# Hash attention and an MLP-mixer on one core: the token stage's last stores, weight chunks and last place

## The chip, the cores and the metric

The kernel runs on one core of a Trainium2 chip, in one launch. The metric is the device time of an execution in microseconds (us). Engines are called PE (TensorE), DVE (VectorE), ACT (ScalarE), POOL (GpSimd) and SP (SyncE, which here only issues DMAs).

## The reference

Four batches, eight heads, 768 positions, 64 features a head, float32. Queries and keys are put into buckets by six sign bits, and a query attends only to the keys of its bucket. The heads are then laid side by side to x (4, 768, 512), and an MLP-mixer follows: a token stage over the positions, and a channel stage over the features.

```python
def _attn_ref(q, k, v, proj):
    ...
    mask = q_bucket[:, :, :, None] == k_bucket[:, :, None, :]
    scores = scale * np.matmul(q, k.transpose(0, 1, 3, 2))
    scores = np.where(mask, scores, -1000000000.0)
    ...
    return np.matmul(attn, v)

def _moe_ref(x, w_tok1, w_tok2, w_ch1, w_ch2):
    xt = x.transpose(0, 2, 1)
    h = np.maximum(xt @ w_tok1, 0.0) @ w_tok2      # 768 -> 256 -> 768
    u = x + h.transpose(0, 2, 1)
    h2 = np.maximum(u @ w_ch1, 0.0) @ w_ch2        # 512 -> 1536 -> 512
    return (u + h2)
```

## The kernel before, in words

**Attention** (0 to 290 us) goes over 16 pairs of heads, four a batch. Its result is `XT`, the residual: 128 partitions, four blocks of features, 4 × 768 positions. The token stage also needs x with the positions on the partitions. So each pair's result is transposed by DVE and written to a DRAM buffer of its batch, `bounced[b]`, by `bounce` (L228): two transposes (L233) and four stores on SP's queue (L238). `fetch(b, x)` (L243) reads a batch back, on SP too (L245). There are two tiles for it: `x0` for batches 0 and 2, `x1` for 1 and 3. Most pairs are stored while attention still runs. The last pair of batch 2 is stored by `bounce_late` (L972) at the very end of attention, from a tile `raw`; on SP these four stores stand between `fetch_turned` (L929) and the fetch of `x1` for batch 1. The last pair of batch 3 is stored at the start of the token stage.

**The token stage** (`tokens`, 290 to 368 us) runs this for each batch b:

- `mix1(b)`: two times six matmuls of 128x512 (L1211) give relu(xᵀ·w_tok1), copied out of PSUM by ACT with the relu (L1218) to `r1`; behind each of the two, one `job()`.
- at b = 0, `weight_sums` (L1188 to L1191), and for every b `left_sums(b)` (L1234 to L1237): sums on DVE for the second product.
- from b = 1 on, the second product of the batch before, in two parts: `mix2(b-1, 0)`, a `job()`, `mix2(b-1, 1)`. Behind the loop come `mix2(3, 0)`, the first two sums of the channel stage (`inputs(0, T, 0)`, L1163 and L1164) and `mix2(3, 1)`.

`mix2(b, m)` (L1240) is one level of Strassen's scheme in seven products (L1251, 128x384), which PE writes to four PSUM banks. ACT copies four of the results to SBUF (L1256, L1259, L1261, L1263), and five adds on DVE (L1266 to L1270) finish the part in a *place*: `places` are three stretches of the weight buffer `second1`, taken in turn by `(2*b+m+1) % 3`. POOL then issues a DMA that adds the place to `XT` in memory (L1271, the accumulate-DMA, 768 KB). A place may be written again when its accumulate-DMA has read it.

A `job()` is mostly a *chunk*: one piece of the channel stage's weights, given as pairs of 32-bit words, is turned into float32 (`Conversion.one`): ACT L177, DVE L187, L191, L195, L196 and L206, and then SP fetches a further piece (L169). The tile `size` that L177 writes has two buffers, so that the L177 of a chunk waits for the L206 of the chunk two before. The first job makes weight sums on DVE (L1301 to L1306).

**The channel stage** (`channels`, 368 us to the end) takes three blocks of 1024 positions; `hidden(s, t)` (L1338 and on) makes a sixth of the hidden layer of a block, again in seven products. Its PSUM tiles `b0` to `b3` are two banks each. In a `hidden`, the first products go to `b0` or `b2` and its neighbour; ACT copies the first result (L1344), and PE then adds a third product to the same bank. DVE's L1378 and L1379 make `R0` from it, then DVE and POOL work on sums for later blocks (L1843 to L1846, the like of L1301 to L1306, and L1382 on POOL), and a last copy by ACT (L1344, the fourth) is followed by three adds (L1387) and L1353.

The order of each engine's instructions is the order in which the code issues them; a tile pool decides which buffer or bank a new tile takes, and puts in the waits for its earlier users. `x0` lies in SBUF over a stretch that the channel stage uses again for `R0` and `R1`; `x1` lies over tiles of attention that its last matmuls (L470) read.

Of the kernel before, what the change touches and what calls it, by code (L numbers as in the profile page):

```python
# [36 lines left out]
F32 = mybir.dt.float32  # L37
# [11 lines left out]
def kernel(  # L49
# [16 lines left out]
    nc = tc.nc  # L66
    P = 128
    B, NP, _, _, S = qk.shape
# [25 lines left out]
    NREG = B * NP - len(SORTED)  # L94
# [46 lines left out]
    class Conversion:  # L141
# [14 lines left out]
        def fetch(self):  # L156
            if not self.todo:
                return
            w, dst, rows, j, n = self.todo.pop(0)
            cols = NW // rows  # L160
            wv = (w.bitcast(U32) if double else w).rearrange("(j p) c -> p j c", p=P)
            src = wv[:, j : j + rows, NE * n : NE * (n + cols)]
            to = dst[:, j : j + rows, n : n + cols]
            if not double:
                nc.sync.dma_start(out=to, in_=src)
                self.fetch()
                return
            raw = self.pool.tile([P, NW, 2], U32, name="raw", tag="raw", bufs=self.bufs)
            nc.sync.dma_start(out=raw.rearrange("p (t n) w -> p t (n w)", t=rows), in_=src)  # L169
            self.fetched.append((raw, to, rows))  # L170
# [54 lines left out]
    dram = ctx.enter_context(tc.tile_pool(name="dram", bufs=1, space=bass.MemoryType.DRAM))  # L225
    bounced = [dram.tile([S, DM], F32, name=f"bounced{b}") for b in range(B)]

    def bounce(stage, n):  # L228

        b, hp = pairs[n]  # L230
        stage = stage.rearrange("p (a k i) -> p a k i", k=2, i=32)
        for k in range(2):
            nc.vector.transpose(  # L233
                stage[:, :, k], XT[:, hp + k, S * b : S * b + S].rearrange("p (a i) -> p a i", i=32),
            )
        to = bounced[b].rearrange("(a i) (g c) -> g i a c", i=32, g=4)
        for g in range(4):
            nc.sync.dma_start(  # L238
                out=to[g, :, :, 32 * hp : 32 * hp + 64],
                in_=stage[32 * g : 32 * g + 32].rearrange("p a k i -> p a (k i)"),  # L240
            )
# [5 lines left out]
    def turn(b, x, bank):  # L247

        for r in range(0, NR, 2):
            ps = bank()  # L250
            for k in range(2):
                at = S * b + P * (r + k)
                for cb in range(NCB):
                    nc.tensor.transpose(ps[:, k, P * cb : P * cb + P], XT[:, cb, at : at + P], ident)
            nc.scalar.copy(x[:, r : r + 2], ps)


    def attention(pool, psum, W1, W2, x0):
# [320 lines left out]
        n = 2 * W * SLOTS  # L579
# [15 lines left out]
        for name, w in widths.items():  # L595
            made[name] = sorting[:, sum(a.shape[1] for a in made.values()) :][:, :w]
        upto, every, pick = (made[name].bitcast(BF16) for name in ("upto", "every", "pick"))
        group_of, groups, place, beyond, spread, some, work, copy, least = (
            made[name]
            for name in ("group_of", "groups", "place", "beyond", "spread", "some", "work", "copy", "least")  # L600
        )
# [369 lines left out]

        def bounce_late():  # L972
            raw = pool.tile([P, NW, 2], U32, name="raw", tag="raw", bufs=2)
            bounce(raw.rearrange("p n w -> p (n w)").bitcast(F32), NREG - 4)

        at(NREG - 1, "newton", bounce_late)
        at(NREG - 1, "begin", fetch_turned)
# [192 lines left out]
    def tokens(pool, psum, W1, W2, x0, weights, jobs, T, places):  # L1170

        x1 = pool.tile([P, NR, DM], F32, name="x1", tag="x1", bufs=1)
        R1 = {}
        turned = not jobs
        if not turned:
            fetch(1, x1)  # L1180
            jobs = jobs(weights(pool))
            bounce(places[2], NREG - 2)
        NQ = DM // 2
        sums = pool.tile([P, 3, HALF], F32, name="W2sums", tag="W2sums", bufs=1)
        b00, b01, b10, b11 = (W2[:, k, HALF * n : HALF * n + HALF] for k in range(2) for n in range(2))

        def weight_sums():
            nc.vector.tensor_tensor(sums[:, 0], b01, b00, op=ALU.subtract)  # L1188
            nc.vector.tensor_tensor(sums[:, 1], b11, sums[:, 0], op=ALU.subtract)
            nc.vector.tensor_tensor(b01, b11, b01, op=ALU.subtract)  # L1190
            nc.vector.tensor_tensor(sums[:, 2], b10, sums[:, 1], op=ALU.subtract)  # L1191

        def job():
            if not turned and jobs:
                jobs.pop(0)()

        def bank(name):
            return psum.tile([P, 512], F32, name=name, tag="mm", bufs=4 if turned else 8)

        def banks():  # L1200
            return psum.tile([P, 2, 512], F32, name="trp", tag="tr", bufs=2)

        def mix1(b):
            x = (x0, x1)[b % 2]
            if b and turned:
                turn(b, x, banks)
            r1 = pool.tile([P, NJ, DM], F32, name="r1", tag="r1", bufs=2)
            for j in range(NJ):
                ps = bank("t1")
                for r in range(NR):  # L1210
                    nc.tensor.matmul(  # L1211
                        ps, W1[:, r, P * j : P * j + P], x[:, r], start=(r == 0), stop=(r == NR - 1),
                    )
                to = r1[:, j]
                if not turned:
                    to = to.rearrange("p (c g i) -> p g c i", c=NCB, i=32)
                    ps = ps.rearrange("p (g c i) -> p g c i", c=NCB, i=32)
                nc.scalar.activation(to, ps, ACT.Relu)  # L1218
                job()
            if b % 2:  # L1220
                new = pool.tile([P, 3, NQ], F32, name="r1s", tag="r1s", bufs=1)
            else:
                new = T[0].rearrange("p k t -> p (k t)")[:, : 3 * NQ].rearrange("p (i c) -> p i c", i=3)
            R1[b] = r1, new
            if not turned and b + 2 < B:
                fetch(b + 2, x)

        def left_sums(b):
            r1, new = R1[b]
            a00, a01, a10, a11 = (  # L1230
                r1[:, k].rearrange("p (m i c) -> p i m c", m=2, i=2)[:, i] for i in range(2) for k in range(2)
            )
            new = new.rearrange("p i (m c) -> p i m c", m=2)
            nc.vector.tensor_tensor(new[:, 1], a00, a10, op=ALU.subtract)  # L1234
            nc.vector.tensor_tensor(a10, a10, a11, op=ALU.add)
            nc.vector.tensor_tensor(new[:, 0], a10, a00, op=ALU.subtract)
            nc.vector.tensor_tensor(new[:, 2], a01, new[:, 0], op=ALU.subtract)  # L1237

        def mix2(b, m):

            r1, new = R1[b]
            a00, a01, s1, a11 = (
                r1[:, k, P * (2 * m + i) : P * (2 * m + i) + P] for i in range(2) for k in range(2)
            )
            new = new[:, :, P * m : P * m + P]
            ps = [bank("t2")[:, :HALF] for _ in range(4)]
            to = places[(2 * b + m + 1) % 3].rearrange("p (i n t) -> p i n t", i=2, n=2)
            p1, u, p7, p57 = (to[:, i, n] for i in range(2) for n in range(2))

            def product(at, left, right, start=True):  # L1250
                nc.tensor.matmul(  # L1251
                    ps[at], left, right, start=start, stop=True, skip_group_check=True,
                )

            product(0, a00, b00)
            nc.scalar.copy(p1, ps[0])  # L1256
            product(1, a01, b10)
            product(2, s1, sums[:, 0])
            nc.scalar.copy(p57, ps[2])  # L1259
            product(3, new[:, 1], b01)  # L1260
            nc.scalar.copy(p7, ps[3])  # L1261
            product(0, new[:, 0], sums[:, 1], False)
            nc.scalar.copy(u, ps[0])  # L1263
            product(2, new[:, 2], b11, False)
            product(3, a11, sums[:, 2], False)
            nc.vector.tensor_tensor(p1, ps[1], p1, op=ALU.add)  # L1266
            nc.vector.tensor_tensor(p57, p7, p57, op=ALU.add)
            nc.vector.tensor_tensor(p57, p57, u, op=ALU.add)
            nc.vector.tensor_tensor(p7, ps[3], u, op=ALU.add)
            nc.vector.tensor_tensor(u, ps[2], u, op=ALU.add)  # L1270
            nc.gpsimd.dma_start(  # L1271
                out=XT[:, 2 * m : 2 * m + 2, S * b : S * b + S], in_=to.rearrange("p i n t -> p i (n t)"),
                accum_op=ALU.add,
            )

        for b in range(B):
            mix1(b)
            if b == 0:
                weight_sums()
            left_sums(b)  # L1280
            if b:
                mix2(b - 1, 0)
                job()
                mix2(b - 1, 1)
        mix2(B - 1, 0)
        inputs(0, T, 0)
        mix2(B - 1, 1)
        while not turned and jobs:
            job()
# [926 lines left out]
    n = NHT // 4 * P  # L2216
# [139 lines left out]
```

## Time and profile before

| what | value |
|---|---|
| device time, median of three runs (lowest to highest) | 768.44 us (768.34 to 770.82) |
| the profiled execution: device time, span | 768.42 us, 766.7 us |
| TensorE's granted clock, mean | 0.999 |
| busy share of the span: PE, DVE, ACT, POOL | 99%, 88%, 58%, 24% |
| token stage, from its first to its last matmul | 289.90 to 368.4 us |

The span is the time from the first to the last instruction; 1.7 us of the execution lie around it. Rows of the profile give the start and the length in us, the engine and line, the operation, output<-inputs with the shapes, and xN where N instructions are put together. A bracket shows how long the engine was idle ahead of it and what ended that. Matmuls are pipelined, so that rows of PE overlap a little. Lines are those of the kernel before; from L1245 on the changed kernel's are three higher.

### The profile page before, as it was taken

To read this page: it belongs to the slowest core of one execution; us is meant where nothing else is said; L and a number is where in the kernel's file an instruction comes from. 1 tells how busy PE (TensorE), PEld (TensorE's weight loads), DVE (VectorE), ACT (ScalarE), POOL (GpSimd) and SP (SyncE) were. 2 spreads that over 40 slices of the span, in tenths; PEclk is the share of its full clock that TensorE was granted. 3 is DMA by queue.
4 is the path that set the end of the run, shared out by engine and by line. 5 is a ranking of instruction groups with operands and counts; after the bars stand their busy time and mean duration, and the time that the engine had idled before them with its cause. 6 is when DMAs were issued, how large, how long until landed. Compare 5 with 4: busy or idle time off the path is not lost.

```text
span 766.7 us, 14567 instructions
## 1 busy us (share of the span) xinstructions
PE 759.4 (99%) x5549; PEld 509.4 (66%) x5549; DVE 672.9 (88%) x965; ACT 444.5 (58%) x820; POOL 185.0 (24%) x258
## 2 busy tenths in 40 slices
PE   9999999999999999999999999999999999999997
PEld 4555655665656554455444468888877888886886
DVE  5899899999998888999788798998899799889884
ACT  6677777677777763334232326566766666665331
POOL 2346772647761700011220100100000011000001
PEclk9999999999999999999999999999999999999999
DMA  7746587674955548886696997899576696750555
GB/s 256 272 170 178 175 245 221 209 205 142 227 191 117 170 64 250 303 189 113 112 327 232 350 354 268 245 242 270 175 221 210 232 261 138 240 158 7 204 159 133
DMA packets 131210, 157.80 MB, mean 206 GB/s; under 512 B 56000, under 2 KB 99520, under 8 KB 129216
## 3 DMA queue, kind: packets, MB, share of 16 engines
q1 hardware_dynamic: 119248, 136.05, 55.9%
q0 software_dynamic: 11600, 20.53, 13.2%
q8 instruction: 45, 0.74, 0.4%
q10 hardware_dynamic: 288, 0.25, 0.1%
q14 instruction: 29, 0.24, 0.1%
HBM read 107.71 MB, written 40.67 MB: 194 GB/s over the span
## 4 chain that ended last, share of the span: by engine, by line
PE 84%; DVE 10%; ACT 2%; issue 1%; DMA 1%; POOL 1%; DVEq 0%; SPq 0%; ACTq 0%; POOLq 0%
PE b L1338 51%; PE sc L503 14%; PE acc L470 12%; PE sc L425 1%; PE hash L536 1%; PE ss L848 1%; DVE size L196 1%; ACT exps L414 1%; DVE unit L195 1%; PE sacc L874 1%; DMA XT<-second 1%; DVE esd L459 1%; DVE second L206 1%; DVE size L191 1%; PE ssums L862 1%
## 5 line engine op out<-in xcount | busy, mean ns | idle before, releaser
L414 ACT ACTIVATE exps<-sc 128x768 f32<-128x768 f32 (+1 forms) x181 | 126.7, 765 | 9.3 <-PE sc L503 6.6
L1338 PE MATMUL b<-R,second 128*128 128x256 f32 (+1 forms) x522 | 131.8, 408 | 0.0
L503 PE MATMUL sc<-qk 32*128 32x384 f32 (+1 forms) x1352 | 119.6, 457 | 0.0
L1338 PEld LDWEIGHTS b<-R,second 128*128 128x128 f32 x522 | 99.1, 190 | 28.5 <-issue 16.5
L470 PE MATMUL acc<-exps,vn 128*32 128x385 f32 (+1 forms) x1344 | 113.2, 486 | 0.0
L503 PEld LDWEIGHTS sc<-qk 32*128 32x128 f32 x1352 | 92.1, 185 | 16.6 <-issue 4.4
L470 PEld LDWEIGHTS acc<-exps,vn 128*32 128x32 f32 x1344 | 44.7, 109 | 62.7 <-issue 59.7
L1344 ACT COPY c<-b 128x256 f32<-128x256 f32 (+1 forms) x96 | 40.3, 426 | 79.4 <-PE b L1338 66.1
L376 POOL DMA_DIRECT2D bits<-XT x104 | 54.5, 526 | 71.2 <-issue 38.8
L459 DVE TENSOR_TENSOR esd<-esd,exps 128x768 f32<-128x768 f32 x70 | 66.9, 956 | 4.3
L1338 PE MATMUL b<-XT,WC 128*128 128x256 f32 (+1 forms) x208 | 61.0, 428 | 0.0
L791 POOL DMA_INDIRECT table<-XT,sorting x48 | 56.4, 1175 | 14.9 <-issue 13.5
L2048 POOL DMA_DIRECT2D out<-second x7 | 8.5, 1212 | 187.3 <-DVE second L2042 81.6
L1338 PEld LDWEIGHTS b<-XT,WC 128*128 128x128 f32 x208 | 39.5, 190 | 15.4 <-issue 10.3
L503 PE MATMUL sc<-bits 32*128 32x384 bf16 (+1 forms) x338 | 48.0, 311 | 0.1
L557 ACT COPY rec<-rec 32x384 f32<-32x384 f32 x56 | 28.5, 510 | 32.6 <-DVE rec L551 31.1
L1338 PE MATMUL b<-XT,SW 128*128 128x256 f32 (+1 forms) x164 | 47.0, 410 | 0.0
L455 DVE TENSOR_TENSOR esd<-esd,exps 128x768 f32<-128x768 f32 x42 | 40.2, 958 | 4.4
L1211 PE MATMUL t<-x,W 128*128 128x512 f32 x96 | 42.1, 594 | 0.1
L1338 PEld LDWEIGHTS b<-XT,SW 128*128 128x128 f32 x164 | 31.1, 190 | 9.4 <-issue 4.1
L1271 POOL DMA_DIRECT2D XT<-second x8 | 9.9, 1234 | 103.5 <-DVE unit L187 63.8
L1211 PEld LDWEIGHTS t<-x,W 128*128 128x128 f32 x96 | 18.1, 190 | 23.1 <-issue 21.7
(331 smaller groups left out, 1449.1 us busy)
## 6 DMA issues: line engine op xcount, KB each, us to landing
second<-left SPq DMA_DIRECT2D x20, 768.0 KB
qk<-in_qk_rows SPq DMA_DIRECT2D x13, 1152.0 KB
raw<-in_moe_w_ch SPq DMA_DIRECT2D x16, 768.0 KB
second<-left SPq DMA_DIRECT2D x18, 576.0 KB
WC<-hidden_left SPq DMA_DIRECT2D x18, 448.0 KB
x<-bounced SPq DMA_DIRECT2D x4, 1536.0 KB
XT<-second POOLq DMA_DIRECT2D x8, 768.0 KB
seen<-in_qk SPq DMA_DIRECT2D x15, 384.0 KB
```

Source lines behind the costliest of these rows:

```text
L376: nc.gpsimd.dma_start(out=to[at : at + 2 * BITS, half[j]], in_=g[of : of + 2 * BITS])
L414: return nc.scalar.activation(e[:, :, columns], sc, ACT.Exp, scale=SCALE)
L455: nc.vector.tensor_tensor(self.d, self.d, e, op=ALU.add)
L459: nc.vector.tensor_tensor(self.d, self.d, e, op=ALU.add)
L470: made = nc.tensor.matmul(acc[D * i + d : D * i + d + 32], vn[:, i, c, d : d + 32], e[:, i], start=(c == 0), stop=(c == NR - 1),)
L503: nc.tensor.matmul(made[j, piece][:, i], k[at : at + 32, ks], q[at : at + 32], start=part < 0, stop=part == 1,)
L557: nc.scalar.copy(rec[other : other + 32, h], rec[at : at + 32, h])
L791: nc.gpsimd.indirect_dma_start(out=tables[2 * w + i], out_offset=bass.IndirectOffsetOnAxis(ap=self.at[:, x : x + 1], axis=0), in_=row, in_ ...
L1211: nc.tensor.matmul(ps, W1[:, r, P * j : P * j + P], x[:, r], start=(r == 0), stop=(r == NR - 1),)
L1271: nc.gpsimd.dma_start(out=XT[:, 2 * m : 2 * m + 2, S * b : S * b + S], in_=to.rearrange("p i n t -> p i (n t)"), accum_op=ALU.add,)
L1338: nc.tensor.matmul(ps, left(k), right(k), start=start and k == ks[0], stop=stop and k == ks[-1], skip_group_check=True,)
L1344: nc.scalar.copy(c, ps)
```

## The change

Three edits. The four stores of `bounce_late` are issued on POOL's queue and not on SP's. The `job()` between the two parts of a second product moves behind both. And the last part, `mix2(3, 1)`, takes the tile `x0` as its place, a fourth one; `x0` is last read by `mix1(2)`.

```diff
-    def bounce(stage, n):
+    def bounce(stage, n, queue=nc.sync):
...
         for g in range(4):
-            nc.sync.dma_start(
+            queue.dma_start(
                 out=to[g, :, :, 32 * hp : 32 * hp + 64],
...
-            bounce(raw.rearrange("p n w -> p (n w)").bitcast(F32), NREG - 4)
+            bounce(raw.rearrange("p n w -> p (n w)").bitcast(F32), NREG - 4, nc.gpsimd)
...
-            to = places[(2 * b + m + 1) % 3].rearrange("p (i n t) -> p i n t", i=2, n=2)
+            place = places[(2 * b + m + 1) % 3]
+            if b + 1 == B and m:
+                place = x0.rearrange("p r c -> p (r c)")[:, : 2 * S]
+            to = place.rearrange("p (i n t) -> p i n t", i=2, n=2)
...
             if b:
                 mix2(b - 1, 0)
+                mix2(b - 1, 1)
                 job()
-                mix2(b - 1, 1)
         mix2(B - 1, 0)
         inputs(0, T, 0)
         mix2(B - 1, 1)
```

**On SP**, at the end of attention, the difference of the two programs (the rows are line, operation, output<-input, shape and count; `bounced_90` is batch 2, `x_3793` is `x1`):

```order
 L918 DMA bounced_91<-XT 128x6x32 x4
 L929 DMA stage<-bounced_91 32x24x32 x8
-L238 DMA bounced_90<-raw 32x24x64 x4
 L245 DMA x_3793<-bounced_89 128x6x512
 L169 DMA raw<-in_moe_w_ch 128x3x512 x2
```

The four stores are gone from ahead of the fetch of `x1`; they stand on POOL between its last gather of attention and the first accumulate-DMA. The fetch of `x0` for batch 2 waits for all four of them.

**On ACT**, from the end of part (0,0) to the first copy of part (1,0), before (`size` and `raw` are the tiles of a chunk, `t2` PSUM banks, `second1` the places):

```order
L177 ACTIVATE size_3910<-raw_3863 128x768
L1256 COPY second1_3784<-t2_3920 128x384
L1259 COPY second1_3784<-t2_3922 128x384
L1261 COPY second1_3784<-t2_3923 128x384
L1263 COPY second1_3784<-t2_3920 128x384
L1218 ACTIVATE r1_3941<-t1_3942 128x4x4x32
L177 ACTIVATE size_3950<-raw_3881 128x768
L1218 ACTIVATE r1_3941<-t1_3960 128x4x4x32
L177 ACTIVATE size_3968<-raw_3918 128x768
L1256 COPY second1_3784<-t2_3982 128x384
```

The same stretch now:

```order
L1259 COPY second1_3784<-t2_3910 128x384
L1262 COPY second1_3784<-t2_3912 128x384
L1264 COPY second1_3784<-t2_3913 128x384
L1266 COPY second1_3784<-t2_3910 128x384
L177 ACTIVATE size_3931<-raw_3863 128x768
L1218 ACTIVATE r1_3941<-t1_3942 128x4x4x32
L177 ACTIVATE size_3950<-raw_3881 128x768
L1218 ACTIVATE r1_3941<-t1_3960 128x4x4x32
L177 ACTIVATE size_3968<-raw_3939 128x768
L1259 COPY second1_3784<-t2_3982 128x384
```

The first L177 has moved behind the four copies of part (0,1). On DVE its five operations stand behind the five adds of (0,1) accordingly. The last L177 here still stands ahead of the copies of (1,0), and it is the one that waits for the L206 of the chunk that moved.

**On DVE**, from the token stage's end to the channel stage's first `hidden`, before (`TA` and `TB` hold the channel stage's sums):

```order
L1163 TENSOR_TENSOR TA_3782<-XT_81 128x1024
L1164 TENSOR_TENSOR TA_3782<-XT_81 128x1024
L1266 TENSOR_TENSOR second1_3784<-t2_4128,second1_3784 128x384
L1267 TENSOR_TENSOR second1_3784<-second1_3784 128x384
L1268 TENSOR_TENSOR second1_3784<-second1_3784 128x384
L1269 TENSOR_TENSOR second1_3784<-t2_4130,second1_3784 128x384
L1166 TENSOR_TENSOR TB_4160<-XT_81,TA_3782 128x1024
L1270 TENSOR_TENSOR second1_3784<-t2_4129,second1_3784 128x384
L1168 TENSOR_TENSOR TB_4160<-XT_81,TB_4160 128x1024
L1378 TENSOR_TENSOR R0_4161<-b0_4168,c_4178 128x2x256
```

And now:

```order
L1163 TENSOR_TENSOR TA_3782<-XT_81 128x1024
L1164 TENSOR_TENSOR TA_3782<-XT_81 128x1024
L1269 TENSOR_TENSOR x0_110<-t2_4128,x0_110 128x384
L1270 TENSOR_TENSOR x0_110<-x0_110 128x384
L1271 TENSOR_TENSOR x0_110<-x0_110 128x384
L1272 TENSOR_TENSOR x0_110<-t2_4130,x0_110 128x384
L1273 TENSOR_TENSOR x0_110<-t2_4129,x0_110 128x384
L1166 TENSOR_TENSOR TB_4160<-XT_81,TA_3782 128x1024
L1168 TENSOR_TENSOR TB_4160<-XT_81,TB_4160 128x1024
L1381 TENSOR_TENSOR R0_4161<-b0_4168,c_4178 128x2x256
```

The five adds of part (3,1) work in `x0`, and the fifth now stands ahead of the wide sum L1166. The tile `b0` of the first `hidden` takes a PSUM bank that the fifth add reads (the bank of `t2_4129`); before, it took banks of part (3,0). L1381, which writes `R0`, waits in the built program for the accumulate-DMA that reads `x0`; before, it waited for no accumulate-DMA.

## Prediction

> **What bounds the kernel now.** I read the page first, then the chain of waits, then the timelines of TensorE (PE), ScalarE (ACT), VectorE (DVE), GpSimd (POOL) and SyncE through the token stage, from 289.9 to 368.4 us. Lines are numbered as in the kernel before. The page's busy shares, and two pieces of the chain around the end of the token stage (start, length, what):
>
> ```profile
> PE 759.4 (99%) x5549; PEld 509.4 (66%) x5549; DVE 672.9 (88%) x965; ACT 444.5 (58%) x820; POOL 185.0 (24%) x258
> ```
>
> ```profile
> 359.37 6.41 DMA XT<-second
> ...
> 368.58 31.76 PE b L1338 x74
> ```
>
> TensorE is busy 99% of the span: a change can win only TensorE's short stalls, and loses what it adds to them. The 6.41 us of an accumulate-DMA hold up the last products of the token stage; behind them the channel stage starts, in which 74 matmuls follow each other without a gap. The stalls are found by comparing equal pieces of TensorE's timeline (start, length, line, operation, count):
>
> ```profile
> 288.52 1.45 PE L470 MATMUL acc<-exps,vn 128*32 128x384 f32 x13
> 289.90 21.25 PE L1211 MATMUL t<-x,W 128*128 128x512 f32 x48
> 311.00 1.45 PE L1251 MATMUL t<-W,r 128*128 128x384 f32 x4
> 315.51 1.45 PE L1251 MATMUL t<-W,r 128*128 128x384 f32 x4
> 320.31 10.46 PE L1211 MATMUL t<-x,W 128*128 128x512 f32 x24
> 330.61 1.45 PE L1251 MATMUL t<-W,r 128*128 128x384 f32 x4
> 333.19 0.81 PE L1251 MATMUL t<-W2sums,r1s 128*128 128x384 f32 x2
> 363.48 1.45 PE L1251 MATMUL t<-W,r 128*128 128x384 f32 x4
> 368.42 3.60 PE L1338 MATMUL b<-XT,WC 128*128 128x512 f32 x8
> 375.29 1.88 PE L1338 MATMUL b<-TB,SW 128*128 128x512 f32 x4
> 380.44 1.02 PE L1338 MATMUL b<-XT,WC 128*128 128x512 f32 x2
> ```
>
> One first product, 24 matmuls, takes 330.61 − 320.31 = 10.30 us; the first two take 311.00 − 289.90 = 21.10, so 0.50 is a stall, where x1 is awaited. The second product of part (b=0, m=0) takes 315.51 − 311.00 = 4.51, part (0,1) 320.31 − 315.51 = 4.80 (0.29 too much), part (3,1) 368.42 − 363.48 = 4.94 (0.43 too much). ScalarE shows the reasons (the bracket is its idle time and what ended it):
>
> ```profile
> 316.92 0.93 ACT L177 ACTIVATE size<-raw 128x768 f32<-128x768 f32 x1 [2.02 <-DVE second L206]
> 331.30 0.92 ACT L177 ACTIVATE size<-raw 128x768 f32<-128x768 f32 x1
> 332.11 0.47 ACT L1256 COPY second<-t 128x384 f32<-128x384 f32 x1
> 365.85 0.48 ACT L1256 COPY second<-t 128x384 f32<-128x384 f32 x1 [2.98 <-DMA XT<-second]
> 377.99 0.58 ACT L1344 COPY c<-b 128x512 f32<-128x512 f32 x1 [1.42 <-DVE R L1378]
> 396.14 0.58 ACT L1344 COPY c<-b 128x512 f32<-128x512 f32 x1 [1.98 <-PE b L1338]
> ```
>
> In (0,1) a weight chunk's L177 waits for DVE's L206 and holds the copy L1256 behind it; in (3,1) the copy waits until the third place back has been accumulated. The three stalls sum to 0.50 + 0.29 + 0.43 = 1.22 us, 0.16% of the time. That is the most that the change can win.
>
> **The change, part by part.** The durations are those of the profiled execution, 768.42 us (span 766.7); the median of the runs is 768.44, so no correction is due.
>
> First, the stores on GpSimd. SyncE loses four issues ahead of the fetch of x1:
>
> ```profile
> 288.15 3.11 SPq L238 DMA_DIRECT2D bounced<-raw  x4
> 291.44 1.01 SPq L245 DMA_DIRECT2D x<-bounced  x1
> 305.34 0.68 SPq L245 DMA_DIRECT2D x<-bounced  x1
> ```
>
> That fetch may not start until the last attention matmul is done at 288.52 + 1.45 = 289.97, since x1 lies over tiles that it reads; so it gains 291.44 − 290.0 = 1.4 us at most, enough for the 0.50. The fetch of x0 for b=2 now waits for GpSimd's four stores, and stands on SyncE ahead of two weight chunks. GpSimd has nothing else to do there, as its first accumulate-DMA shows (58 us idle ahead of it):
>
> ```profile
> 325.69 1.35 POOL L1271 DMA_DIRECT2D XT<-second  x1 [58.26 <-DVE unit L187]
> ```
>
> No row shows such a store on GpSimd; the nearest is this issue of 1.35 us, and four of them from 288.15 end at 293.6, almost twelve us before SyncE comes to that fetch at 305.34. I cost it at nothing; its dear end is a rival.
>
> What the gain is worth is decided behind it, by DVE, whose rows stand end to end through this stretch. I quote the second of the left sums, the adds of (0,0), the chunk behind them and the adds of (0,1):
>
> ```profile
> 311.62 0.42 DVE L1235 TENSOR_TENSOR r<-r 128x256 f32<-128x256 f32 x1
> 322.43 0.55 DVE L1266 TENSOR_TENSOR second<-t,second 128x384 f32<-128x384 f32 x1
> 324.61 0.56 DVE L1270 TENSOR_TENSOR second<-t,second 128x384 f32<-128x384 f32 x1
> 325.08 0.55 DVE L187 TENSOR_SCALAR unit<-size 128x768 uint32<-128x768 uint32 x1
> 329.00 0.55 DVE L1266 TENSOR_TENSOR second<-t,second 128x384 f32<-128x384 f32 x1
> ```
>
> The third product of (0,0) needs L1235, which ends at 312.04 and is tied to DVE's queue; TensorE reaches that product four matmuls on, at 311.00 + (333.19 − 330.61) / 2 = 312.29. So it can come 0.25 earlier and no more; half of the 0.50 is lost at once.
>
> Second, the chunk behind both parts. The wait in (0,1) goes (0.29). Five adds take 325.08 − 322.43 = 2.65 us from start to start, a chunk 329.00 − 325.08 = 3.92. With (0,1)'s adds ahead, the chunk's L206 ends at about 325.08 + 2.65 + 3.92 = 331.65 instead of 329.0. With two `size` buffers, the L177 of the chunk two later can't start sooner; it stands on ScalarE just ahead of the copies of (1,0). Before, it started at 331.30 and the copy at 332.11; now the copy is at 331.65 + 0.81 = 332.46 or a little later, however early TensorE arrives. What is won until then, at most 0.25 + 0.29 = 0.54, is thus mostly taken back here: TensorE writes that bank again at 333.19, and can't before the copy ends, 332.46 + 0.47 = 332.93, or with the late start and the step to TensorE about 333.1. Net −0.1 for both parts; the bounds are −0.79 (all won) and 0.
>
> Third, the fourth place. The wait of 2.98 us on ScalarE goes, and with it 0.43 on TensorE. But two other waits come with it. In the built program PSUM's banks turn: before, the four of (3,1) were none that the channel stage's first matmul writes; now one of them is, and it is read last by L1270 of (3,1). The first matmul of the channel stage waits for that add. DVE's rows there:
>
> ```profile
> 365.88 1.22 DVE L1164 TENSOR_TENSOR TA<-XT 128x1024 f32<-128x1024 f32 x1
> 367.02 0.55 DVE L1266 TENSOR_TENSOR second<-t,second 128x384 f32<-128x384 f32 x1
> 370.70 1.21 DVE L1168 TENSOR_TENSOR TB<-XT,TB 128x1024 f32<-128x1024 f32 x1
> ```
>
> The adds start at 367.02 straight behind L1164, so earlier copies don't start them earlier. In the new order all five stand together, 367.02 + (324.61 + 0.56 − 322.43) = 367.02 + 2.74 = 369.76. The channel stage begins there and not at 368.42: **+1.33**, with the 0.43 inside it. DVE's two wide sums behind them, L1166 and L1168 (1.2 us each), then end near 372.2, ahead of the matmuls that read TB (375.29 before).
>
> The other wait: x0 lies under the channel stage's R0, so DVE's first add there, L1378, waits until the accumulate-DMA has read x0. GpSimd's rows, and then DVE's from there:
>
> ```profile
> 379.62 1.21 POOL L1271 DMA_DIRECT2D XT<-second  x1 [5.59 <-DVE seen L1844]
> 380.37 1.76 POOL L1382 TENSOR_TENSOR c<-c 128x512 f32<-128x512 f32 x1
> ```
>
> ```profile
> 377.26 0.69 DVE L1378 TENSOR_TENSOR R<-b,c 128x512 f32<-128x512 f32 x1 [5.35 <-ACT c L1344]
> 379.97 2.58 DVE L1846 TENSOR_TENSOR seen<-SW,seen 128x384 f32<-128x384 f32 x1
> 384.88 1.75 DVE L1301 TENSOR_TENSOR second<-second 128x1536 f32<-128x1536 f32 x1
> 392.87 0.68 DVE L1378 TENSOR_TENSOR R<-b,c 128x512 f32<-128x512 f32 x1
> ...
> 395.57 0.56 DVE L1846 TENSOR_TENSOR seen<-second,seen 128x384 f32<-128x384 f32 x1
> ...
> 425.34 0.69 DVE L1378 TENSOR_TENSOR R<-b,c 128x512 f32<-128x512 f32 x1 [1.61 <-PE b L1338]
> ```
>
> The accumulate-DMAs follow each other 5.59 + 1.2 = 6.8 us apart, so that data ready at 370 is issued at 379.62; nothing in the change shortens this queue. It lands at 379.62 + 6.41 = 386.03. (The Trainium skill, "DMA: Bandwidth & Descriptors", section "Anatomy of one DMA — SWDGE (gpsimd) path", gives 2.0 us and the bytes over 436 GB/s, by my estimate 3.8 us for these 768 KB, so that the wait would end near 383.4 and the 0.5 below would be nothing; the trace's 6.41 does not agree, and it decides.) So L1378 runs at 386.1 instead of 377.26, 8.8 us late. Behind it on ScalarE stands the last copy of that step (377.99), and behind that the first copy of the next step, which TensorE needs before it writes the same bank. A step takes 380.44 − 368.42 = 12.02, the bank is written 375.29 − 368.42 = 6.87 into one: due at 369.76 + 12.02 + 6.87 = 388.65. The copies are 386.1 + 0.7 + 2 × 0.58 = 387.96: in time, by 0.7. One step on it is tighter. From L1378 to the four weight sums DVE took 384.88 − 377.26 = 7.62, less up to 2.0 if L1846 (2.58 here beside POOL's L1382, 0.56 in the next step) no longer meets GpSimd; the sums took 392.87 − 384.88 = 7.99, less up to 0.9. So the second L1378 comes between 386.1 + 12.7 = 398.8 and 386.1 + 15.6 = 401.7; GpSimd's add now stands behind the late copy too, so I take 399.8. Add 0.7 + 1.16: 401.7, against 369.76 + 24.04 + 6.87 = 400.67. That is 1.0 with the middle value and nothing with the early one; the relief that is likely (one of the two collisions falls away) halves it: **+0.5**, between 0 and 2.9. After that DVE, which has idle time again at 425.34 (1.61 us waiting for TensorE), catches up.
>
> Sum: 768.42 − 0.1 + 1.33 + 0.5 = 770.15, told as **770.1**. Its own range is 769.0 (−0.79, and 0 for the last term) to 771.2 (0 for the first, about +1.4 for the last).
>
> **The rivals.** *All the stalls go and nothing comes* (0.10): the bank's wait is covered and x0's costs nothing. For it: the stalls are real rows, and DVE is late at most points anyway. Against it: L1164's end at 367.1 fixes the adds. Time: 768.42 − 1.22 = 767.2.
>
> *R0's wait reaches TensorE in full* (0.13), the slower end. The place is L1378 of the first two steps. It decides from a landing later than 386.03 + 0.7 = 386.7: every us past that is one on TensorE; and with both collisions kept, the second step alone costs 2.9. For it: the queue of accumulate-DMAs is full, and SyncE's stores of the weights start in the same stretch. Against it: the collision that goes, and DVE's idle time later. Time: 768.42 − 0.1 + 1.33 + 2.9 = 772.5.
>
> *The four stores land late* (0.12). They are small, scattered packets, and if each takes as long as the accumulate-DMAs are apart, 6.75 us, the last lands at 288.1 + 27 = 315.1; the fetch of x0 comes behind that. The fetch of x1, of the same size, was issued at 291.44 and awaited until about 300.2 + 0.5 = 300.7, 9.3 us with other loads beside it; so x0 lands by 324.4 at the worst, and TensorE needs it at 320.3: up to 4 late, and 2 as the middle, since SyncE's other loads here stand behind it. For it: no row shows these stores, and DVE is busy all through. Against: GpSimd's issues beside a busy DVE took 1.2 to 1.35 us. Time: about 2 on top, 772.1. The Trainium skill ("SBUF — State Buffer", section "SBUF: two separate sides") says that DVE work in a two-port mode keeps GpSimd from writing the descriptors of its own DMAs, and advises SyncE's or ScalarE's queue, the opposite of this edit. No row here shows such a stop; by it the stores would be late as in this rival.
>
> *The change does nothing that shows* (0.04): the built order gives no gain and no wait, 768.4.
>
> **How the numbers follow.** The forecast has 0.61, of which 0.10 lies above 770.75. A measurement of this kernel can tell about 0.3%, 2.3 us, from no change: 766.1 to 770.75. Slower is 0.10 + 0.13 + 0.12 = 0.35; faster has only the first rival's tail, 0.02; the rest, 0.63, is the same. The range leaves out most of the first rival and half of the two slow ones: 767.6 to 772.2.
>
> **What would show it.** Right: the gap at 300 gone; no wait of L177 in (0,1), but one of it ahead of (1,0); the first channel matmul released by the last add of (3,1), 1.3 us after the last token matmul could have ended; L1378 at about 386 released by the DMA, and at most a short stall on TensorE at 388 or 400. Wrong: the first channel matmul straight behind the token stage; a stall over 1.5 us on TensorE in the channel stage's first three steps; a wait for x0 at 320.

## The result and the profile after

The changed kernel takes 774.59 us (median of six runs, 774.3 to 775.8), the kernel before 768.31 (six runs, 767.83 to 770.82): the ratio is 1.0078, with a 95% interval of 1.0067 to 1.0088. It is slower by 6 us; the forecast was 770.1, with a range up to 772.2. The profiled execution took 775.8 us with a span of 774.1, 7.4 more than the span before. TensorE's timeline, cut at the same places as before, says where the 7.4 lie (lines from L1245 on are three higher now):

```profile
290.78 20.87 PE L1211 MATMUL t<-x,W 128*128 128x512 f32 x48
311.48 1.45 PE L1254 MATMUL t<-W,r 128*128 128x384 f32 x4
315.62 1.62 PE L1254 MATMUL t<-W2sums,r 128*128 128x384 f32 x2 [2.69 <-DVE r L1235]
...
320.33 1.45 PE L1254 MATMUL t<-W,r 128*128 128x384 f32 x4
...
324.85 10.46 PE L1211 MATMUL t<-x,W 128*128 128x512 f32 x24
...
368.02 1.45 PE L1254 MATMUL t<-W,r 128*128 128x384 f32 x4
...
374.35 3.70 PE L1341 MATMUL b<-XT,WC 128*128 128x512 f32 x8 [1.65 <-DVE x L1273]
...
386.47 3.60 PE L1341 MATMUL b<-XT,WC 128*128 128x512 f32 x8
...
463.98 4.12 PE L1341 MATMUL b<-R,second 128*128 128x256 f32 x18 [0.49 <-ACT c L1347]
...
511.97 2.32 PE L1341 MATMUL b<-XT,WC 128*128 128x256 f32 x10
```

The last row begins the second block of positions; before, it stood here:

```profile
505.21 2.32 PE L1338 MATMUL b<-XT,WC 128*128 128x256 f32 x10
```

| piece | before | after | difference |
|---|---|---|---|
| up to the first token matmul | 289.90 | 290.78 | +0.88 |
| first products of batches 0 and 1 | 21.10 | 20.70 | −0.40 |
| part (0,0) | 4.51 | 8.85 | **+4.34** |
| part (0,1) | 4.80 | 4.52 | −0.28 |
| from there to part (3,1) | 43.17 | 43.17 | 0 |
| part (3,1), to the first channel matmul | 4.94 | 6.33 | **+1.39** |
| channel stage to its second block of positions | 136.79 | 137.62 | +0.83 |
| the rest, to the last instruction | 261.49 | 262.13 | +0.64 |

The first row lies in attention, which the change does not touch; in the runs below the token stage starts anywhere between 289.3 and 292.3. The difference in the last row arises behind TensorE's last matmul. Without these two, the change cost 5.88 us in this execution.

Part (0,0) is new. TensorE waits 2.69 us for L1235, the second of the left sums on DVE. DVE's rows show why that is late:

```profile
308.30 0.96 DVE L196 TENSOR_TENSOR size<-size,unit 128x768 f32<-128x768 f32 x1
311.73 0.96 DVE L206 SCALAR_TENSOR_TENSOR second<-raw,size 128x768 uint32<-128x768 uint32 x1 [2.47 <-DMA bounced<-raw]
...
315.05 0.42 DVE L1235 TENSOR_TENSOR r<-r 128x256 f32<-128x256 f32 x1
```

Before, the same L206 followed its L196 without a wait:

```profile
308.30 0.96 DVE L206 SCALAR_TENSOR_TENSOR second<-raw,size 128x768 uint32<-128x768 uint32 x1
```

Now L206 of the first chunk waits 2.47 us for the stores of `bounce_late`. It doesn't read what they store: it is the first to write the weight buffer `second0`, and in SBUF that buffer covers part of the tile `raw` from which the stores read. The stores are late because GpSimd issues them far apart:

```profile
289.61 0.80 POOL L238 DMA_DIRECT2D bounced<-raw  x1 [21.67 <-DVE raw L233]
293.12 0.74 POOL L238 DMA_DIRECT2D bounced<-raw  x1 [2.71 <-issue]
299.82 0.72 POOL L238 DMA_DIRECT2D bounced<-raw  x1 [5.96 <-issue]
305.72 0.72 POOL L238 DMA_DIRECT2D bounced<-raw  x1 [5.17 <-issue]
```

Each issue takes 0.7 to 0.8 us, but 2.7 to 6.0 us of waiting that no semaphore explains stand ahead of the last three, and the last store lands at 311.6.

The gap of 2.69 us costs 4.34. The table of stretches has the rest (us, then busy time of PE, PEld (TensorE's weight loads), DVE, ACT and POOL, then TensorE's granted clock, DMA share, GB/s):

```profile
313.00:315.60 2.60, 0.00 (x0) 0.01 (x1) 2.50 (x7) 0.99 (x2) 0.00 (x0) 0.90 0.73 275
315.60:317.00 1.40, 1.38 (x2) 0.83 (x3) 1.33 (x4) 0.00 (x0) 0.00 (x0) 0.50 1.02 380
317.00:318.30 1.30, 1.30 (x3) 0.67 (x2) 1.30 (x2) 0.48 (x1) 0.00 (x0) 0.50 1.03 388
318.30:320.30 2.00, 2.00 (x7) 1.23 (x6) 1.93 (x4) 0.96 (x2) 0.00 (x0) 0.96 0.75 288
```

Behind the gap the granted clock is 0.50 for nearly 3 us, in which the matmuls take twice as long: 2.69 + 1.65 = 4.34. The Trainium skill ("TensorE: Matmul & The Clock Gate", section "Part 1: The HAM clock gate (the "warmup" mystery)") gives half the clock after an idle window of about 3.4 us; here 2.69 us were enough.

The wait for the last add of (3,1) came as forecast. So did DVE's wait for the accumulate-DMA that reads `x0`:

```profile
389.56 0.69 DVE L1381 TENSOR_TENSOR R<-b,c 128x512 f32<-128x512 f32 x1 [12.87 <-DMA XT<-x]
```

### The profile page after: what moved, and what is told of

Its sections match the earlier page's. It is cut to its first block, busy times and chain, and to the rows that moved or that the text cites. A ratio compares the mean times of both kernels' runs of the same rounds, so it can differ in the third digit from the quotient of the medians.

```text
span 774.1 us, 14571 instructions
## 1 busy us (share of the span) xinstructions
PE 761.5 (98%) x5549; PEld 508.9 (66%) x5549; DVE 669.8 (87%) x965; ACT 445.1 (58%) x820; POOL 187.1 (24%) x262
## 4 chain that ended last, share of the span: by engine, by line
PE 90%; DVE 4%; issue 2%; DMA 1%; POOL 1%; ACT 1%; DVEq 0%; SPq 0%; POOLq 0%
PE b L1341 51%; PE sc L503 13%; PE acc L470 12%; PE t L1254 4%; PE t L1211 3%; PE sc L425 1%; PE hash L536 1%; PE ss L848 1%; PE sacc L874 1%; DMA bounced<-raw 1%; DVE esd L459 1%; PE hash L348 1%; PE ssums L862 1%; POOL bits L376 1%; DVE esd L455 0%
## 5 line engine op out<-in xcount | busy, mean ns | idle before, releaser
L791 POOL DMA_INDIRECT table<-XT,sorting x48 | 56.2, 1172 | 15.2 <-issue 14.1
L908 POOL DMA_INDIRECT XT<-result,sorting x24 | 26.6, 1107 | 7.5 <-issue 6.9
```

What stands on the lines that cost most here:

```text
L791: nc.gpsimd.indirect_dma_start(out=tables[2 * w + i], out_offset=bass.IndirectOffsetOnAxis(ap=self.at[:, x : x + 1], axis=0), in_=row, in_ ...
```

## The experiments

Theory A after this trace: the loss is the sum of waits with separate causes, namely stores that land late and hold L206, and a PSUM bank that holds the first channel matmul. The rivals were that the stores only cost together with the moved chunk, that the bank's wait belongs to another edit than the prediction said, and, for the stores, that GpSimd is slow for another reason. All ratios are to the kernel before on the same chip, with 95% intervals.

### The three edits one by one, and the two without the stores

The edits are those of the change: `e1_stores` has the stores on GpSimd alone, `e2_jobs` the moved chunk alone, `e3_place` the fourth place alone, `e4_jobs_place` the last two.

e1_stores: 

> The kernel before with only the four stores on GpSimd. Theory A: the last of these stores lands at about 311.6, and DVE's L206 of the first chunk may not write the second weight buffer until they have read the tile raw that lies under it. So DVE idles about 2.5 us there, TensorE waits about 2.7 us for L1235, its granted clock falls for a few us behind that gap, and the time is 3.5 to 4.3 us above the kernel before. Rival B: the wait only bites together with the moved chunk; then the stores alone win x1's 0.5 us and the time is 0 to 0.5 us below.

e2_jobs: 

> The kernel before with only the chunk moved behind both parts. Theory A: it is this edit, and not the fourth place, that turns the PSUM banks; the first channel matmul then waits for the last add of part (3,1), L1270, which here stands behind L1166 and ends at 370.8 in the trace of before, so that the time is about 370.8 - 368.4 = 2.4 us less at most 0.4, 2.0 to 2.4 us above before. Rival B: the bank wait belongs to the fourth place, as the prediction had it; then this run is 0 to 0.3 us below before.

e3_place: 

> The kernel before with only the fourth place. Theory A: the banks stay as before, so that TensorE goes straight on into the channel stage and wins the 0.43 us of part (3,1); DVE's L1381 waits for the accumulate-DMA until about 386 without a stall on TensorE there, and at most one late copy in the first outputs costs 0.7 us: -0.4 to +0.3 us. Rival B: the bank wait comes with the place: +1.3 us or more.

e4_jobs_place: 

> The changed kernel with the four stores back on SyncE. Theory A: without the stores' 4.0 us, what is left is the wait of the first channel matmul for L1273 (+1.3), and perhaps the late copy in the first outputs (+0.7): 1.2 to 2.1 us above before. Rival B: all of the loss comes from the stores: 0 to 0.8 us below before.

| run | ratio | token stage, first token to first channel matmul (before: 78.52 us) |
|---|---|---|
| e1_stores | 1.0043 (1.0029 to 1.0057) | 81.65 |
| e2_jobs | 1.0054 (1.0040 to 1.0067) | 80.99 |
| e3_place | 1.0046 (1.0033 to 1.0060) | 78.10 |
| e4_jobs_place | 1.0037 (1.0023 to 1.0051) | 79.95 |

The stores alone cost 3.3 us: the same wait for L1235 as in the changed kernel, with a clock of 0.50 behind it.

```profile
314.57 1.62 PE L1251 MATMUL t<-W2sums,r 128*128 128x384 f32 x2 [2.36 <-DVE r L1235]
```

Theory A's mechanism holds. The time is a little under its range; in the trace the late stage also spares TensorE the wait for a place in (3,1), 0.42 us.

With the chunk alone the first channel matmul waits for the last add of part (3,1):

```profile
371.52 3.70 PE L1338 MATMUL b<-XT,WC 128*128 128x512 f32 x8 [2.25 <-DVE second L1270]
```

So it is the chunk's move that turns the banks, and not the fourth place; in the built program of `e3_place` the banks are those of before. The wait is longer than in the changed kernel, because L1270 here stands behind the wide sum L1166. The token stage grew by 2.47; the ratio stands for 4.2 us, above theory A's 2.0 to 2.4, and over 1 us of that is in no row that I could name.

The fourth place alone was the surprise: theory A expected −0.4 to +0.3 us, rival B the bank's wait, and neither came. TensorE goes straight on into the channel stage, 0.42 us sooner than before, and then stalls in its second and third step:

```profile
367.96 3.60 PE L1341 MATMUL b<-XT,WC 128*128 128x512 f32 x8
...
379.98 3.60 PE L1341 MATMUL b<-XT,WC 128*128 128x512 f32 x8
...
388.06 1.98 PE L1341 MATMUL b<-TB,SW 128*128 128x512 f32 x4 [1.05 <-ACT c L1347]
...
393.32 3.60 PE L1341 MATMUL b<-XT,WC 128*128 128x512 f32 x8
...
401.77 1.98 PE L1341 MATMUL b<-TB,SW 128*128 128x512 f32 x4 [1.42 <-ACT c L1347]
...
407.02 3.60 PE L1341 MATMUL b<-XT,WC 128*128 128x512 f32 x8
```

The two steps take 13.34 and 13.70 us instead of 12.02, 3.0 more. Both stalls wait for ScalarE's copies, and these for DVE and the accumulate-DMA:

```profile
386.21 0.69 DVE L1381 TENSOR_TENSOR R<-b,c 128x512 f32<-128x512 f32 x1 [14.10 <-DMA XT<-x]
```

That is the prediction's second rival, in another kernel than it was made for. In the changed kernel the channel stage starts later, by the stores' loss and the bank's wait, while the accumulate-DMAs move by less (the last is issued at 383.00, in `e3_place` at 379.65): the wait for R0 ends 389.56 − 374.35 = 15.2 us after the first channel matmul instead of 386.21 − 367.96 = 18.3, and the copies are in time. One wait hid the other. The bank's wait alone is enough for that: in `e4_jobs_place` R0's wait ends 385.71 − 369.27 = 16.4 us after the first channel matmul, and the first three steps take 12.12, 12.02 and 12.09 us.

Without the stores (`e4_jobs_place`) there are the bank's wait of 1.65 us and 0.77 us in the first outputs, where DVE is still late; the time, 2.8 us by the ratio, is above theory A's range, though its interval reaches down to 1.8. The sum of the three single edits, 3.3 + 4.2 + 3.5 = 11.0 us, is not the change's 6; the stores alone and the other two edits together make 3.3 + 2.8 = 6.1, which is.

### What makes the stores late

`e5_act` issues the four stores on ScalarE's queue, `e6_two` two of them on GpSimd and two on SyncE, and `e7_long` has GpSimd write the same bytes in long runs to a buffer that nothing reads. Batch 2 then gets batch 0's x, so `e7_long` does not compute the reference's result; only its times are used. The lines are cut from the differences to `e1_stores`:

```diff
-            bounce(raw.rearrange("p n w -> p (n w)").bitcast(F32), NREG - 4, nc.gpsimd)
+            bounce(raw.rearrange("p n w -> p (n w)").bitcast(F32), NREG - 4, nc.scalar)   # e5_act
...
-            queue.dma_start(
+            (queue if g < 2 else nc.sync).dma_start(   # e6_two
...
+            if queue is nc.gpsimd:   # e7_long
+                queue.dma_start(out=aside[32 * g : 32 * g + 32], in_=stage[32 * g : 32 * g + 32].rearrange("p a k i -> p (a k i)"))
+                continue
...
-        nc.sync.dma_start(out=x, in_=bounced[b].rearrange("(r p) c -> p r c", p=P))   # fetch, e7_long
+        nc.sync.dma_start(out=x, in_=bounced[0 if b == 2 else b].rearrange("(r p) c -> p r c", p=P))
```

e5_act: 

> The kernel before with the four stores on ScalarE's queue. Theory A (what counts is how late DVE comes to the left sums, not which queue is used): the four issues, 3 us in the trace of before, stand ahead of ScalarE's last work for attention, DVE's chain behind it moves by up to 3 us, L1235 ends at about 314 to 315 and TensorE waits 2 to 2.6 us for it, with 1 to 1.6 us of lower clock behind: 2.5 to 4 us above before, though no store is late. Rival B (GpSimd's queue alone is at fault): x1's wait goes and nothing comes: 0 to 0.5 us below before.

e6_two: 

> The kernel before with two of the four stores on GpSimd and two left on SyncE. Theory A (each store on GpSimd holds up the next by 3 to 7 us, and only the late end of the last one costs time): the second is issued at about 292.5 and lands by about 299, long before L206 needs it at 308.3; x1's wait shrinks; -0.6 to +0.2 us. Rival B (every store on GpSimd lands late, whatever their number): L206 waits again, +1.5 us or more.

e7_long: 

> The kernel before with four stores on GpSimd that write the same bytes in long runs, 32 of 6 KB each instead of 768 of 256 bytes, to a buffer of their own; batch 2's x is read from batch 0's buffer instead, in the same size. Theory A (the gaps between the stores come from the number of their pieces, which GpSimd's queue can hold only so many of): issues about 0.8 to 1 us apart, the last landed by 296, no wait of L206, 0 to 0.6 us below before. Rival B (each DMA on GpSimd waits until the one before has landed, or DVE's work holds it up): issues still 3 to 7 us apart and L206 waits, +2.5 to 4 us.

`e5_act` is slower, 1.0062 (1.0046 to 1.0078), without a late store. That is 4.8 us, above theory A's 2.5 to 4; its token stage, 82.73 us, is 4.2 longer than before. The issues stand ahead of ScalarE's last work for attention, and DVE's chain, which waits for that, moves on by about 3 us:

```profile
288.01 3.15 ACTq L238 DMA_DIRECT2D bounced<-raw  x4
291.20 0.16 ACT L479 COPY vsum<-acc 128x1 f32<-128x1 f32 x1 [3.39 <-issue]
```

```profile
315.42 1.62 PE L1251 MATMUL t<-W2sums,r 128*128 128x384 f32 x2 [3.51 <-DVE r L1235]
```

So it is DVE's arrival at L1235 that counts, whatever makes it late. `e6_two` is as fast as before (1.0000, 0.9991 to 1.0009): two stores on GpSimd land in time. In `e7_long` (1.0005, 0.9996 to 1.0015) GpSimd issues all four one behind the other:

```profile
289.42 2.08 POOL L240 DMA_DIRECT2D aside<-raw  x4 [21.69 <-DVE raw L234]
```

With few, long pieces there is no wait between issues, beside the same work on DVE. So the gaps come with the number of pieces. The time is as before, and not 0 to 0.6 us below, as theory A had it. Whether GpSimd is slow to write many descriptors or has no room for them was still open. The kernel gives their memory 1024 bytes a partition. `e9_ring` doubles it:

```diff
-        "TRN2", target_bir_lowering=False, num_devices=1, dynamic_dma_scratch_size=1024
+        "TRN2", target_bir_lowering=False, num_devices=1, dynamic_dma_scratch_size=2048
...
-            return len(seen) == 3 or not unseen and seen
+            return len(seen) == 2 or not unseen and seen
```

e9_ring: 

> The run with only the stores on GpSimd, and the memory for GpSimd's DMA descriptors doubled from 1024 to 2048 bytes a partition (to make room, the check of the inputs in the channel stage looks at two tiles in turn and not three, and one weight sum there uses another tile). Theory A (this memory holds the descriptors of little more than one such store, and the next must wait until they are used up): the first two issues stand about 1 us apart, the others follow within some 3 us, the last store has landed by 303, L206 waits for nothing, x1's wait is gone: -0.5 to +0.5 us against before. Rival B (GpSimd is slow at writing many descriptors, or DVE's work keeps it from it): gaps of 3 to 7 us as before, L206 waits, +3 us.

The waits left the token stage (78.63 us long, L206 without a wait), but the time stayed at 1.0046 (1.0034 to 1.0059): the side edits put new waits into the outputs, 0.8, 0.5 and 1.8 us. A further execution of the same kernel (773.58 us) had the same issues within 0.3 us.

e12_ring_before: 

> One look more at the run with the stores on GpSimd and 2048 bytes for descriptors, to see whether the places and times of its issues repeat: the same gaps within 1 us.

`e13_ring` makes the room more gently, and `e15_base` has that room without the change:

e13_ring: 

> Only the stores on GpSimd, and 2048 bytes a partition for GpSimd's DMA descriptors. Room for them is made in the channel stage: one of three tiles of the check of the inputs holds 512 of the 768 columns (the last third of those inputs is not checked), and one set of weight sums is stored in three pieces. Theory A (descriptor memory): issues as in the first run with 2048 bytes, no wait for L1235, token stage about 78.6 us long as before, time within 0.8 us of before. Rival B (the loss is in the stores on GpSimd, whatever their waits): +2.5 us or more.

e15_base: 

> The kernel before with 2048 bytes for descriptors and the room for them made in the same way, without any part of the change. Theory A (the side edits are harmless, and only accumulate-DMAs come earlier, which takes away the 0.43 us of part (3,1) at most): within 0.6 us of before. Rival B (the side edits cost time in the outputs): +1 us or more, and the other three runs are to be read against this one.

`e15_base` is at 0.9991 (0.9980 to 1.0003), `e13_ring` at 0.9998 (0.9987 to 1.0010), 1 us above `e15_base` by the medians (769.75 and 768.77), which the two intervals don't tell apart. So with double the memory most of the 3.3 us is gone, and what is left can't be told from nothing:

```profile
289.96 1.56 POOL L238 DMA_DIRECT2D bounced<-raw  x2 [19.12 <-DVE raw L233]
293.57 0.72 POOL L238 DMA_DIRECT2D bounced<-raw  x1 [2.05 <-issue]
296.95 0.73 POOL L238 DMA_DIRECT2D bounced<-raw  x1 [2.66 <-issue]
```

The same stores, beside the same DVE work, now stand 3.5 us apart or less. L206 has no wait, and the token stage takes 78.66 us. So GpSimd waits for descriptor memory. The stop by DVE's port that the Trainium skill ("SBUF — State Buffer", section "SBUF: two separate sides") warns of is not what made the stores late here.

### The bank and the place

`e10_banks` mends the bank in the kernel with the chunk alone; `e8_x1` takes `x1`, which lies under R1, as the fourth place in the kernel before (the lines of `e10_banks` are against `e2_jobs`, those of `e8_x1` against `e3_place`):

```diff
-            product(1, a01, b10)
-            product(2, s1, sums[:, 0])
+            early = [lambda: product(1, a01, b10), lambda: product(2, s1, sums[:, 0])]   # e10_banks
+            for one in reversed(early) if not turned and b + 1 == B and m else early:
+                one()
...
-                place = x0.rearrange("p r c -> p (r c)")[:, : 2 * S]
+                place = x1.rearrange("p r c -> p (r c)")[:, : 2 * S]   # e8_x1
```

e10_banks: 

> The run with only the chunk moved, and in part (3,1) the third product issued ahead of the second, so that the PSUM bank that the first channel matmul takes is read by the first of the five adds and not by the last. Theory A (the 2.4 us in that run are the wait for this one bank): the wait of 2.2 us goes, the token stage is as long as before or 0.3 us shorter, -0.3 to +0.3 us against before. Rival B (TensorE waits for DVE's end whatever the bank, through b1 or TB): a wait of 1 us or more in the first channel step, +1 us or more.

e8_x1: 

> The kernel before with the tile x1 as the fourth place instead of x0. In the program R1 lies over it and not R0, so that DVE waits for the accumulate-DMA at its fifth-last add of the first step (382.5 in the trace of before) and not at L1378 (377.3). Theory A (in the run with x0 as the place the 3.0 us of stalls come from that wait alone, through the two copies on ScalarE behind it): the wait shrinks from 9 to about 3.6 us, no copy is late, TensorE has no stall in the first steps: 0.3 to 0.5 us below before, or up to 0.3 above if the first outputs still wait. Rival B (any fourth place costs, since DVE cannot make up for a wait): +1 us or more.

`e10_banks` is at 0.9998 (0.9988 to 1.0008), its token stage 78.55 us long: the 2.25 us are gone with the bank. Part (0,1) wins its 0.29, and part (1,0) takes 4.84 instead of 4.51, which is the give-back by L177 that the prediction described. `e8_x1` is at 1.0004 (0.9994 to 1.0014). The stalls behind `x0` shrink from 3.0 to 0.5 us, but the first outputs wait for DVE, so that the 0.42 won in the token stage is spent:

```profile
399.16 1.98 PE L1341 MATMUL b<-TB,SW 128*128 128x512 f32 x4 [0.22 <-ACT c L1347]
...
458.33 4.12 PE L1341 MATMUL b<-R,second 128*128 128x256 f32 x18 [0.92 <-DVE R L1994]
```

### The whole change, mended

`e11_all` is the changed kernel with both mends and the room made as in `e9_ring`; `e14_all` has the gentler room, and `e16_after_ring` the descriptor memory alone.

e11_all: 

> The changed kernel with both mends: 2048 bytes for GpSimd's descriptors, and the product order of part (3,1). Theory A (the three waits were all of the loss, and the accumulate-DMAs too stand 6.7 us apart only for want of descriptor memory, so that the last one lands early enough for R0): the three stalls of before are gone and nothing new comes, -1.2 to -0.2 us against before. Rival B (the accumulate-DMAs are that far apart because their transfers take as long): L1381 waits until about 386 again and TensorE stalls about 3 us in the second and third channel step, as in the run with only the fourth place: +1.5 to +2.5 us.

e14_all: 

> The changed kernel with 2048 bytes for descriptors (room made as in e13_ring) and the product order of part (3,1) that frees the bank early. Theory A: no stall of over 0.4 us from the end of attention to the last hidden step, token stage about 78.1 us long, time between 1.0 us below and 0.4 us above before. Rival B (DVE stays late because of R0's wait or of the moved chunk, and the first outputs pay): +1 us or more, with waits for DVE in the first outputs.

e16_after_ring: 

> The changed kernel with 2048 bytes for descriptors only. Theory A: only the bank's wait for the last add of part (3,1) is left, 1.65 us in the trace of the changed kernel: 1.3 to 2 us above e14_all. Rival B (with the accumulate-DMAs early, DVE is early too and the bank's wait goes by itself): within 0.5 us of e14_all.

`e11_all` is at 1.0054 (1.0039 to 1.0069), far above theory A's range. Like `e9_ring`, it loses this in the outputs alone (gaps of 2.56, 1.54, 0.28 and 1.73 us); every channel step of its first block takes 12.02 us. `e14_all` is at 0.9989 (0.9977 to 1.0001): the whole 0.8% is gone. Its accumulate-DMAs, 6.7 to 6.8 us apart before where several follow each other, are issued down to 2.6 us apart, and R0's wait ends 10.6 us after the first channel matmul (at 369.22):

```profile
379.86 0.69 DVE L1382 TENSOR_TENSOR R<-b,c 128x512 f32<-128x512 f32 x1 [6.49 <-DMA XT<-x]
```

Its token stage, 78.13 us, is 0.4 shorter than before; as to the time, it can't be told from `e15_base` (0.9991), nor from the kernel before. `e16_after_ring` is at 1.0013 (1.0000 to 1.0025), 2 us above `e14_all` by the medians (771.01 and 769.05), with the one wait that is left:

```profile
369.74 0.70 PE L1341 MATMUL b<-XT,WC 128*128 128x512 f32 x1 [1.65 <-DVE x L1273]
```

## Why the prediction was wrong

- **Bounds.** Right: TensorE without gaps, stalls of 1.22 us to win, and no more.
- **The stores on GpSimd** is the step that failed. It took four issues of 1.35 us, end to end, from the accumulate-DMA's row, and said that they end at 293.6. The same prediction read, further on, that accumulate-DMAs follow each other only 6.8 us apart, and the 5.59 us of idle time that it read there was the same wait: with double the descriptor memory the accumulate-DMAs stand down to 2.6 us apart (`e14_all`). The third rival used it and put the last landing at 315.1 (311.6 measured), but with a chance of 0.12. And both named the wrong victim. They looked at who reads what the stores write, the fetch of x0 at 320, which was never late; the wait came from the bytes that the stores read, which `second0` takes over, 11 us sooner. The cost was 4.3 us, of which 1.65 were lost clock, an item that no part of the sum had. Without the stores (`e4_jobs_place`) the change costs 2.8 us (1.8 to 3.9) against the 1.7 that the sum gives, so that the 3.3 us of the stores are the larger part of the miss.
- **x1's wait.** The first products won 0.40. The prediction let half of the 0.50 be lost at once to DVE's left sums; where nothing else was late (`e13_ring`, `e14_all`, `e16_after_ring`), part (0,0) took 4.9 instead of 4.51, so nearly all of it was.
- **The chunk behind both parts.** Right where it was worked out: the wait in (0,1) goes, and (1,0) gives 0.33 back, as the kernel with the chunk alone shows. In the changed kernel TensorE was late by then, so nothing was given back.
- **The bank's wait.** Its size was right, 1.39 for 1.33, since the bank was read from the built program of the whole change; its owner was wrong. It came with the chunk's move (`e2_jobs` has it, `e3_place` does not).
- **R0's wait.** Forecast at +0.5 in the third channel step. In the changed kernel it was nothing there and 0.73 in the first outputs: "DVE catches up" did not hold. The rival's wait is real: 3.0 us in `e3_place`, where nothing ahead of it delays the channel stage. That this is close to the rival's 2.9 is luck: the rival had it in one step, for a channel stage that starts at 369.76, and `e3_place` has 1.3 and 1.7 in two steps, for one that starts at 367.96.

## What to carry to other kernels

When a transfer is moved to another queue, ask for both ends: who waits for what it writes, and who takes over the memory that it reads from. Idle time ahead of a DMA's issue can be a price and not free time, whether the row puts it down to "issue" or, as the 5.59 us here, to an engine that has nothing to do with it; look for it in the queue's own rows before costing further DMAs there. And when several edits each add a wait, price each alone and then in the order of time: a wait ahead can hide one behind it, and the sum of the parts says little.

## What the runs showed of the hardware

- GpSimd issues its DMAs as far as the descriptor memory lasts. With 1024 bytes a partition, four stores of 768 pieces stood 3.5 to 7.0 us apart (the changed kernel and `e1_stores`); with 2048 bytes 3.9 us or less (`e9_ring`, `e13_ring`); with 32 pieces each, 0.5 us on average (2.08 us for four, `e7_long`). Accumulate-DMAs of 768 KB that were ready waited with 1024 bytes and stood 6.7 to 6.8 us apart; with 2048 in `e14_all` each was issued within 0.7 us of the end of its last add, down to 2.6 us apart.
- A gap of 2.36, 2.69 or 3.51 us on TensorE in the token stage (`e1_stores`, the changed kernel, `e5_act`) was followed by about 3 us at a granted clock of 0.50. A gap of 2.25 us ahead of the first channel matmul was not (`e2_jobs`, 1.00 in the next stretches), nor one of 1.65 there, nor one of 2.56 in the first outputs of `e11_all`. So the length of the gap alone does not decide it; what does is open.
